# A written-out order of a sparse-attention and gMLP kernel replaced by another: order, engines, PSUM banks and transposes

## The chip, the cores and the metric

The kernel runs on one core of a Trainium2 chip. The metric is the device time of one execution in microseconds (us). Each engine (PE for matmuls, DVE, ACT, POOL for elementwise work, SP for starting transfers) takes its own queue of instructions strictly in order, and an instruction waits for those of other engines that it depends on. DMAs are started from queues as well: here from POOL's (loads that cast f32 to f16) and SP's (raw loads, transposing transfers inside SBUF, stores of the output).

## What is computed

Inputs are q, k, v of shape 4 x 8 x 768 x 64 (batch, head, position, width), and the weights of a gated MLP. The reference, cut to what matters:

```python
# attention; chunks of 32 keys, 24 chunks, the best 6 are kept for each query
k_min, k_max = np.min(k_chunks, axis=3), np.max(k_chunks, axis=3)
ub = np.sum(np.maximum(q[:, :, :, None, :] * k_min[:, :, None, :, :],
                       q[:, :, :, None, :] * k_max[:, :, None, :, :]), axis=-1)
ub = np.where(causal, ub, -1000000000.0)
top_chunks = np.argsort(ub, axis=-1)[..., -top_k:]
mask = sel & (pos[:, None] >= pos[None, :])
scores = np.where(mask, scale * np.matmul(q, k.transpose(0, 1, 3, 2)), -1000000000.0)
# softmax of scores, times v, heads put side by side: x of 4 x 768 x 512
h = np.maximum(x @ w_in, 0.0)                 # 512 -> 1024
u, v = h[..., :512], h[..., 512:]
v_n = (v - mu) / np.sqrt(var + 1e-06)
v_s = np.einsum('ts,bsd->btd', w_spatial, v_n) + b_spatial[None, :, None]
out = (u * v_s) @ w_out
```

## The kernel before

**Stages.** The 32 heads are taken as 16 pairs, 0 to 15; four pairs make a batch, two pairs share one "chunk" of loads (four heads of k and v, two loads of q). After every fourth pair the gMLP of that batch is mixed in with the attention of the next pairs. For a pair the stages are:

- `load_ops` (from L385): k, q and v are loaded by POOL's casting DMA (L414). For the first chunk each head of k and q can be loaded instead as raw f32 by SP (L419).
- `chunk_ops` (from L481): k of four heads is transposed to kT, on PE (L500, then a copy out of PSUM) or by one DMA transpose from SP (L488); raw f32 heads go through PE as f32 (L512). DVE takes the largest and smallest key of each chunk (L523, L526, L529).
- `put_ops` (L532): the chunk bounds are spread into km and the keys into kh, by copies on DVE (L249), POOL (L245) or ACT (L243).
- `prep_ops` (L549; `prep_first` for pair 0): q is transposed, on PE (L568) or by a DMA transpose from SP (L577). Two relu make rq, the positive and the negative part of q. If q went through PE, they read PSUM and run on DVE or ACT; if it went through the DMA they read SBUF, and run on DVE (L257, L259), POOL (L255) or ACT (L253). PE then multiplies rq by km: the upper bounds (L590, ten short matmuls). DVE finds the eight largest (L606) and writes a "not selected" mask beside q (L612). q and mask are transposed together to a, on PE (L626) or by DMA from SP (L617).
- `attend_ops` (L692): for each head and each of six strips, scores on PE (L711), exp on ACT (L722), then the causal triangle: added on PE as one more matmul (L714), or cut out afterwards on POOL (L733) or DVE (L731). PE multiplies by v (AV, L742), DVE normalises (L756), and x is transposed, on PE (L773) or by DMA (L766).
- `mlp_ops` (L778), once for each batch: the v half of the first layer (L790, 512 columns), relu, statistics (L796) and normalising (L814) of it, the u half (L832, 384 columns), the spatial product (L848, 384 columns), bias (L852), gates (L857, POOL or DVE), the last layer (L876, 512 columns), copies of it to `o` (ACT L243, DVE L247) and stores (L883). The very last tile of the output is made in two pieces of 256 columns.

**What sets the order.** Nothing is scheduled when the kernel is built. Every stage registers its operations by `s.op(...)`, with its engines to choose from, its PSUM bank if it takes one, and where there are two ways to do a thing, a "when" that belongs to one of them. The table PLAN (from L51) then says in which order they are issued. It is a string read three characters at a time:

```python
            hi, lo, how = (DIGITS.index(x) for x in plan[c:c + 3])
            o = self.ops[64 * hi + lo]
            if o.when is not None:
                assert self.mode.setdefault(o.when[0], o.when[1]) == o.when[1]
...
            if o.take is not None:
                o.take.tile = self.banks[how // 4 - 1]
            if len(o.alts) > 1:
                o.emit(list(o.alts)[how % 4])
```

Two characters name the operation, and the third gives the engine (remainder by 4) and one of eight PSUM banks. Listing one of two ways chooses it. The order of the table is the order on every engine's queue. The table was found by annealing on a planner's prices, which the code still carries beside each operation. The one for rq from SBUF, at L583, gives DVE 0.25, POOL 0.63 and ACT 0.62 us:

```python
                s.op([("DVE", 0.25, 0.37), ("POOL", 0.63, 0.7), ("ACT", 0.62, 0.76)], lambda e, m=m: relu(
                    e, rq[:, m, P:S].rearrange("p (t c) -> p t c", c=P), a[:, 1:NQT, 0, :], 1.0 - 2 * m), key + 0.2,
```

Of the kernel before, what the change touches and what calls it, by code (L numbers as in the profile page):

```python
# [37 lines left out]
def blocks(half):  # L38
# [10 lines left out]

DIGITS = "0123456789ABCDEFGHIJKLMNOPQRSTUVWXYZabcdefghijklmnopqrstuvwxyz+/"  # L50
PLAN = (  # L51
    "0000N10P10K10140I00D00t00S00H00O00o00V00800x00500B00v00600700U01880W10Z00900A00p00T00b00c10R1100"
    "0M00J10a14201200Q00d002C03G0E02dK0Y10z00C01901A00X01J11VO0F01B00w10L01C01KS1I11D01E004W1F02e02n4"
    "2h02j02+22i01hC2l01W11M01G11L04402z11Y01X01a04301f11H12k01g12o11j11Z01c08e01501b01N81i149G47K2r0"
    "1e01O02s02t01d11kO1P01Q01RW2u02m01l02w01m04A12v04811S13212y033S1n01o44J13001tC1y83513411qG4C01+0"
    "2x02/00k04B036K1p02KO4E08f01v04502TW4D02543701s02V04F02QS2S02F82H02CC3804G01/G3904PW5P04Q05WS2N8"
    "3113DK2M04R05Y04H03BO3C02108lG2P03E08jW2704M02E04I05X18k04L04S84T05T03I45S03NO3WC3K022K8g05O03Y0"
    "4K12403TS3V03FW3P05Z43oC3dK8m05U10j04N14U05a03rG3lS4V00G04X83q02JO5b02X0BB04O13H04ZC3n05R14Y03gW"
    "3Q85c05gS3f04a03i01x44jK3S02Y03uC8n02904bW3t08o03w05h04l08q00i0Fg05Q14m82A04o050G8p04zC5eS2Z00e0"
    "8r03MK3a03k84/04pO3b04d08s08u04eC3y05205V14r04g05EW8/G2B05G04sO3z05844u055C5A06IW5f0A9S6K08t03+0"  # L60
    "8+167O6903c0AA04i85r49008x0A508y08z140K5s0570910A204105BW4w00g06FO5D04x05x44y06H095G5y0960A810f0"
    "2bC6LK5jW5k0A10AB05+854O0h09705I08w1A6264SBI46N06CW5/05J08v16605mK9806E09AG9B15K0BJ0BC0AF85n09CO"
    "5uS6X42c09D06BWBGCAG0A715v09gO6P06Y09rGBH15MK5o05N16d46009s05pSA41BD0AH06Q0AI09h06109lC6R0BL09u8"
    "AJ06ZKA316e06208h09m06309v0FlWFm06bGFnO6a06c1BN09o49p09FC9G06f86TS9NW9O06U0ID0Fo0BK0BP09QG6VK6W1"
    "9T49R06iC9dS9e0BW17eWFq0BM076O6nK9WG9X07f09U0Fh0Ch16j06k07g06o0770Fi06g0BO0Ca07806sSFp06l0Fr06t0"
    "6u0BU06p0AqGBY8Ci4B2C7BW7C0B30Cj1ASOBa0AT07SSAnKAo0AXCBE0Ck0Cf0BR0Ce07T0BZ07U0Ar09Y06q07h8BQ0Ft0"
    "9I4BV0Cb0BeO9J06v07i0Fs07D06w0Bf0Cd1APK9w0AQ0CoS9i07VGFu0H806r07W0Cp06m0AY07X0H40714720Bg0730790"
    "6x0Bh07MW7bK7c07j0Cq0BX17N06y07E07407O09jC7A0AyGAz0Bi09x0Fv0AdOAe07Y4Fz0750Aa8Ab07Z07F0AgWAh07G0"
    "9K0Cg19LGCr0Fw06h06z06/06+09Z0BS17d0A/OB007PS7H0F+07007Q0G187a0G307R0Ai07I0AvWHBKAU0H70AVOAs0BT1"
    "Aw07L1Cc19a07J0Aj08747uS880G20HD09b07v0G7WHC1Ak07z8CAGAl07+07K1BoKCs0CB0Bp0BrO9y09z0Bs0G807/0890"  # L70
    "CDGBzCCRKH317w0G90Bt1COOFy0GA0Mi0F/1CE07pGB+07q0BwCB407r0CP0CS0IH0Bx0C/OFx08008HW7s00l0CLKGB08I0"
    "G01810D00CF1CM0C0CC10IE08J0At8CIOCJ0B50C3GC40DNKDO07x0HHC8K07t1B60DSSCT07kWDT0DYO9+0H61HI0DKGB70"
    "DVK7l07m0D48DZ082S8A0830DL0Db4CGOHJ0IN0HK0D50B9GH91HA1CU0IM0DW0DA87n0Dc0Dd1D7CDDKIF0840BA1HM4HN0"
    "CyWC50D80H51DB0BuGC60GSCCz0DE0GH8CV0DP08C47o08D0GtWIP0D10DQKCW0Mm0850Mk0HOOGT0GI0C70DF0De0Gu0C80"
    "HP0IO0GiCGj0GKSHR87y0GqGCX0Df0GYW8E0IQ0GL0GfOGnCDg00m08F0Fj0GZ0Gr0IR0IW0HfSGg0D2WIY1DG0DkKDH0HS0"
    "IT0IaGGo0Gk0DI0GP4GQ0IV1PF0Hg0Ic0DuOJk8Jd2Ib0Jm0HiWHj0Jc0DiCDj0IX1E84IZ1IU1HsGJl1GM0Ht0860DpSIS1"
    "Dv0Jg1IgCE90Ms0Ih0Ii0EjWI18Ek0Dw0Ij0Ik0Jh1GVGDl0Mj0EXOEY0EA0El0Dx0I20Gw4GW0HZWHa0Mu0Gx0Ga0Dm1Dq0"
    "Dr08PCMw08Q0PH0ER8JqGES0HcWH+KHx4GNSET0Hy0Gb0Hd08MCI48EZ18N0Ds0Jr0EgOMr0I50Dt0Js0Jt08B1Ju0Jj18O0"
    "Ji1Hk0Jf18L0Gl4HUWEh0HV0Ei0Je1EDGPJ0EB0EE0IqCEO8H/0Gy1Mt0Gc0Ir0EP0IG0ItWEQ0EF1Dn0J2OJ5KJ60Mv0J30"
    "Gz0I/GG+0M/1EUCMy0HW08G0E38Gd08R0J00Dy0Mx0Do0HpKG/0Hq0EaOJFSEG0IyGJG0E40Iz0Eb0I60N34JCKE51Ec0HXS"  # L80
    "JNGDz0D+0JO0EH0N40Hl0EV0N50EC0JK8Hm0JTOEW0JL08S4O50JU0D/0Hn0E10JD0N00Mz0JQG8T0N9CK9SJR0E60E70Hu0"
    "Hv8I70PG0N11EI0NA0E00K1OK208VKNB0Iu0EJ0OG0I80NC0JV08Y4JH0EdGEe0ND08W0EK0I90E21K6OKA0JIWK70Ef1EL0"
    "JW0EM0E/C8Z1EmKH00KF8ErGPP0Es0PR0PO0J70KaSKCOKG0En0M+1PQ0EN1J+8JX0F44JY0PW1KD0Eo0N21F50Kb0J/0Ep0"
    "F00KMOKdSPT0Ke0PS0KX8F10KN0O90F60KPWKQ0O62KY0Et0KH0K30K4SO818X0OB2IA0EwKEx0Ey0KUOEu0Iv0IwWNR8Eq0"
    "J80NJGKV0Ez0KR0F20FJK8a0J90Pf0JA0KI0OH2NpOJZ0OA2NS0F70NvCPY1Kf0FEWKJ0FF0PZ1KS8Kg0NK0OI1OJ4Qe0Nw0"
    "OC1Nq0NsG8U0KK0Kh0Ki0Kj0FK0FG0NaCOK0F30NXSFL0Nb0NMOOL0F98O71OM0PV1FA0NhCQj2FB0Ph28b4E+0Ev1Nt0NN0"
    "QmGNUOPa1FC0Pb1FM08c0FH0Qo0ON0Pg0Qh1NV0FO8PU2NkKQn1Nl0FP0Ny4FN1LlWKrONz0Qk1Lm0LTGPiKLU0Ln1LV1Km8"
    "Qi2Kn0Qf2Pj0Pk0Pl0Ko1Kp08d0FR4KwWOeGKs0Kt1Ml0NY0P0SQg1P10Of0FS1Kx0OkKL58L60Ni0OTSL70ObGLZOFUCNO0"
    "Oz4Kq0Ol0Oh8PX1Nc0Oc0La0OU0FV0LAKL80LB0N+0Ky1Ql1LQGNm1QsWKz0Oi0O+0Ku0P6SLFCFD0LG0Qt0Lb0LR0Kv0LW8"
    "LX0P70Ou4K+0K/0OrOLH0LC1FI0Qu0L90LD0L00Pm0Qv0Os0LE0OWSNPKOX0OY0Nd0LcCLd0LS1Q4OOv0Le0Q7WL10P3SQ14"  # L90
    "Ne0F80FW0Nf0LfGLg0FT0OZCQ50L20QVKQ80LiOLY1Qw0LI0LJ0Om0NnWN/0QM8P40P80Lj0Lk1QHSL41On0Oo0Op0FQ0QW0"
    "Q20Ow0FXKO00Ps4QN0PvOFd8Lh1QPCLK0L30QI0LL0Pt0QESPI0LM0O10QSGPw0Fe0LP0QT0LN0P+4P/0LO0FY1FaOLy8FZ0"
    "QF0QQ0Q90O20RBWOxGP90PA0Lz0L+0RW4LoSFb0PB0RHCR0KRC0Lp0ROOQX0RX0Px0R3GLq0R10M1WRR4Lr0RI0LtKLs0Lu0"
    "Lv0RS0RP0RECR40RfSRF0RZ4R50R8OQJ1MGGR90Ff0L/0M00Ra0Rc8QKCRd0Lw0RT0QY0RJ0PyKM20QZ0Qa0M30M40Rg0R6O"
    "QA0QB0MB4RK0RL0RU8Rh0QC0M50Ri0Rj0Rk0PC0SCCM6SLx0MH0MLWRoKRM0MM0MN0MO0MP1Ry8MC0M70Qb0MI0MJ0MD0ME0"
    "M80MWOMX1S7WRl0M90MQGSY4RtORu0MR0MY0Rp0Rv0Rq1MA0Rz0Rw0R+0R/0Rr0S00SD0Rx0Rs0SHSSI0SJ1SE0SF0SG0Fc0"
    "S10S20S30SZ0Sa0MS0S80MTGSSOS90SA0S50SB0MF0MK0MfKSK0SL0Sn8So0MU0MZCShSS41Mg0ST0Ma0Mc4MV0SM0SN0SbW"
    "Sc0S60SU0Mb0Mh0T3GSO0SP1SvKSR1SqCSi0Sw0SQ1S+OSr0Sx0Md0Sd1Sy0Sj0SVWSW0Ss0Se4TDST40T50S/0T00SX0St0"
    "Su1SkKTNWSl0T60T10T21TE0Sf0TF0Sp0Sz1TG0TO0T70TP0TSCTT0T88Sg0Sm0T90TH0TQ0TIGTJ0TK0TA0TVOMe0TU0TR1"
    "TYSTW0TL0TB0TZ0TX0Ta0TM0TC1ThWTbCTi0Tj0Tc0Td0Te4Tf0TkKTg0Tl0Tm0"  # L100
)


# [831 lines left out]
```

## Time and profile before

| | |
|---|---|
| runs of before | 194.24, 194.37, 194.5 us; median 194.37 |
| profiled execution, its own time | 194.3 us |
| its span (first to last instruction) | 192.6 us |
| matmuls, starts of two 128-column ones apart (median) | 56 ns |
| first score matmul (L711) starts | 15.68 us |
| last matmul ends; last store issued; landed | 188.98; 189.66; 191.55 us |
| stores of 256 KB, issue to landing | 2.2 us (median) |
| DMA transposes: a<-qs, xT<-x, kT<-kp | 12, 10, 3; 4.3, 2.6, 5.3 us to landing (median) |

How to read the profile: busy time is that of instructions on an engine, as a share of the span. The slices are 40 equal parts of the span, each digit the busy share in tenths; PEclk is the clock that PE was granted, in tenths of full speed. The chain of waits goes back from the last instruction to what released it, step by step. In groups, "out<-in" are the tiles' names, then shapes, how often, busy time and the mean of one in ns, and the idle time just before with what ended it. A timeline line has start, length, engine, line and operation; several instructions in a row are put together with their number.

### The profile page before, as it was taken

The page shows a single profiled execution, that of the slowest core. Times are in us where ns is not written, and L with a number is a line of the kernel's source. Part 1 is how long each engine was busy: PE and PEld are TensorE (multiplying, and loading weights), DVE is VectorE, ACT ScalarE, POOL GpSimd, SP SyncE. Part 2 cuts the span into 40 slices and gives each one's busy share as a digit, 9 for nine tenths or more (in the row PEclk, how much of TensorE's full clock was granted, in tenths as well). Part 3 has the DMA queues.
Part 4 walks back from the last instruction along what each step waited for, and adds up shares of the span by engine and source line. Part 5 has one row for each costly group of instructions (what it writes and reads, how often), then busy time and mean ns, then how long its engine had stood idle before and what let it go on. Part 6 is the DMA issues. An engine that isn't in the chain of part 4 may idle for free.

```text
span 192.6 us, 5740 instructions
## 1 busy us (share of the span) xinstructions
PE 183.5 (95%) x2132; PEld 130.4 (68%) x2132; DVE 157.3 (82%) x549; ACT 153.3 (80%) x326; POOL 129.1 (67%) x215
## 2 busy tenths in 40 slices
PE   7649999999999999999999999999999999999992
PEld 7548999997567677875667667655776775456541
DVE  5978999999699999899999988979987366674840
ACT  8998999999999899898889887849799810596052
POOL 7988899979967949999985478995173560500310
PEclk9975999999999999999999999999999999999999
DMA  8999999999996999999999968689359412423035
GB/s 126 136 153 158 166 148 162 188 175 162 156 127 133 156 197 158 127 150 141 180 213 172 162 188 137 177 85 120 116 134 147 129 38 46 167 99 119 0 122 205
DMA packets 111291, 27.33 MB, mean 142 GB/s; under 512 B 106144, under 2 KB 107680, under 8 KB 111264
## 3 DMA queue, kind: packets, MB, share of 16 engines
q0 software_dynamic: 73904, 11.90, 83.5%
q1 hardware_dynamic: 37360, 15.08, 34.1%
q8 instruction: 16, 0.26, 0.6%
q14 instruction: 11, 0.09, 0.1%
HBM read 24.77 MB, written 6.29 MB: 161 GB/s over the span
## 4 chain that ended last, share of the span: by engine, by line
PE 82%; DVE 8%; ACT 4%; POOL 2%; issue 2%; ACTq 0%; POOLq 0%; DVEq 0%
PE bank L711 18%; PE bank L848 16%; PE bank L876 10%; PE bank L790 10%; PE bank L742 10%; PE bank L832 8%; PE bank L590 2%; PE bank L626 2%; PE bank L568 2%; DVE st L796 2%; POOL kp L414 1%; PE bank L714 1%; ACT kh L243 1%; PE bank L773 1%; PE bank L500 1%
## 5 line engine op out<-in xcount | busy, mean ns | idle before, releaser
L722 ACT ACTIVATE e<-bank 128x512 f16<-128x512 f32 (+2 forms) x192 | 92.6, 558 | 11.2 <-PE bank L711 6.5
L711 PE MATMUL bank<-a,kh 128*128 128x128 f16 (+2 forms) x384 | 58.7, 263 | 0.2 <-DVE x L756 0.2
L711 PEld LDWEIGHTS <-kh 128*128 128x128 f16 x384 | 32.5, 99 | 11.9 <-issue 0.6
L857 POOL TENSOR_TENSOR shared<-tmp,uT 128x384 f16<-128x384 f32 x22 | 20.4, 935 | 28.6 <-DVE tmp L852 28.3
L848 PE MATMUL bank<-wsT,vn 128*128 128x384 f16 x192 | 39.2, 326 | 0.1
L245 POOL COPY kh<-kT 64x384 f16<-64x384 f16 x55 | 29.1, 530 | 7.5 <-PE bank L711 4.6
L733 POOL TENSOR_SCALAR_AFFINE_SELECT e<-e 128x384 f16<-128x384 f16 x44 | 23.3, 542 | 15.4 <-ACT e L722 14.0
L832 PE MATMUL bank<-xT,w_in 128*128 128x384 f16 x128 | 28.5, 326 | 0.1
L742 PE MATMUL bank<-vt,e 128*128 128x65 f16 x672 | 27.4, 193 | 0.0
L742 PEld LDWEIGHTS <-e 128*128 128x128 f16 x672 | 25.0, 97 | 2.3
L790 PE MATMUL bank<-w_in,xT 128*128 128x512 f16 x96 | 25.4, 379 | 0.0
L243 ACT COPY o<-bank 128x512 f32<-128x512 f32 x19 | 11.3, 594 | 17.5 <-PE bank L876 15.6
L876 PE MATMUL bank<-w_out,shared 128*128 128x512 f16 (+1 forms) x100 | 24.0, 371 | 0.1
L852 DVE TENSOR_TENSOR tmp<-bank,bias 128x384 f32<-128x384 f32 x32 | 17.1, 552 | 8.4 <-PE bank L848 6.3
L848 PEld LDWEIGHTS <-vn 128*128 128x128 f16 x192 | 17.1, 98 | 10.0 <-DVE vn L814 0.5
L756 DVE TENSOR_TENSOR x<-bank,rec 128x384 f16<-128x384 f32 x32 | 17.5, 551 | 0.5
L414 POOL DMA_DIRECT2D qs<-in_q_dram x17 | 17.2, 1009 | 0.1
L832 PEld LDWEIGHTS <-w_in 128*128 128x128 f16 x128 | 11.3, 97 | 7.8 <-issue 0.3
L796 DVE BATCH_NORM_STATS2 st<-vraw 128x6 f32<-128x512 f32 x24 | 16.0, 681 | 0.7 <-ACT vraw L253 0.6
L876 PEld LDWEIGHTS <-shared 128*128 128x128 f16 x100 | 9.4, 98 | 9.2 <-DVE shared L857 0.6
L606 DVE MAX8 m<-bank 128x8 f32<-128x8 f32 (+4 forms) x150 | 13.5, 164 | 0.1
L790 PEld LDWEIGHTS <-xT 128*128 128x128 f16 x96 | 8.7, 98 | 7.1
(99 smaller groups left out, 297.4 us busy)
## 6 DMA issues: line engine op xcount, KB each, us to landing
out_dram<-o SPq DMA_DIRECT2D x23, 256.0 KB, 2.2
vt<-in_v_dram POOLq DMA_DIRECT2D x8, 384.0 KB, 7.2
kp<-in_k_dram POOLq DMA_DIRECT2D x7, 384.0 KB, 7.1
qs<-in_q_dram POOLq DMA_DIRECT2D x14, 192.0 KB, 5.4
shared<-in_moe_w_spatial_dram POOLq DMA_DIRECT2D x3, 384.0 KB, 6.2
w_in<-in_moe_w_in_dram POOLq DMA_DIRECT2D x4, 256.0 KB, 6.4
w_out<-in_moe_w_out_dram POOLq DMA_DIRECT2D x2, 256.0 KB, 5.7
vraw<-in_k_dram SPq DMA_DIRECT2D x2, 192.0 KB, 2.7
```

Source lines behind the costliest of these rows:

```text
L245: nc.gpsimd.tensor_copy(o, f)
L414: s.op(("POOL", 0.62 + 0.19 * nh, 0), lambda: nc.gpsimd.dma_start(out=dst(name, h0, nh), in_=src(a, h0, nh)), key, w=w, load=PAIRB * nh / ...
L711: mm(bs.f32[:, col:col + n], lhsT=kh[:, hi, t * P:(t + 1) * P], rhs=a[:, f // P:(f + n) // P, hi, :], start=True, stop=not on)
L722: s.op(("ACT", *act_cost(n)), lambda g=g, n=n, bs=bs, e=e: nc.scalar.activation(out=e[:, BASES[g]:BASES[g] + n], in_=bs.f32[:, 0:n], func= ...
L733: nc.gpsimd.affine_select(out=o, in_=o, compare_op=Alu.is_ge, fill=0.0, base=0, channel_multiplier=-1, pattern=[[0, 3], [1, P]])
L742: mm(o[:, qi, :], lhsT=e[:, c:c + P], rhs=v_r[nv][:, 2 * hi + x, t, 0:D + 1], start=first and n == 0, stop=last and n == len(bl) - 1)
L790: mm(bk.f32, lhsT=x[:, ko, t * P:(t + 1) * P], rhs=w_in_sb[:, ko, DH:DFF], start=(ko == 0), stop=(ko == NDO - 1))
L796: s.op(("DVE", 0.60, 0.74), lambda vraw=vraw, st=st: nc.vector.bn_stats(st, vraw), kk, r=[("vr", nvr[t])], w=[("st", nst)])
L832: mm(bk.f32[:, 0:N], lhsT=w_in_sb[:, ko, db * P:(db + 1) * P], rhs=x[:, ko, c], start=(ko == 0), stop=(ko == NDO - 1))
L848: mm(bk.f32[:, 0:N], lhsT=vn[:, si, db * P:(db + 1) * P], rhs=wsT[:, si, c], start=(si == 0), stop=(si == NQT - 1))
L857: eng.tensor_tensor(gT[:, db, c], in0=tmp, in1=uT[:, db, c], op=Alu.mult)
L876: mm(bo.f32[:, 0:c1 - c0], lhsT=gT[:, db, t * P:(t + 1) * P], rhs=w_out_sb[:, db, c0:c1], start=(db == 0), stop=(db == KO - 1))
```

## The change

Only the string PLAN is replaced, from its first line to its last. No operation, shape, price or function changes; the table stays about as long. The first and last lines of the diff, which has 49 such lines on each side:

```diff
@@ -49,55 +49,55 @@
 PLAN = (
-    "0000N10P10K10140I00D00t00S00H00O00o00V00800x00500B00v00600700U01880W10Z00900A00p00T00b00c10R1100"
-    "0M00J10a14201200Q00d002C03G0E02dK0Y10z00C01901A00X01J11VO0F01B00w10L01C01KS1I11D01E004W1F02e02n4"
+    "0v00000H00N00o00I10140R00S00280V003C0800B00x00501100600C00t00K00M00W00700p04200D02dG0900Y10L00a1"
+    "0b00Z00Q00c01200T00d10P00z00U10O143018K0w22pO0J11911J11VS2e00A02h02j02l02i01KW0E00F00442q11h82k0"
...
```

What the two tables come to, counted on each engine:

| operation | before | after |
|---|---|---|
| K transposes on PE (L500); f32 ones (L512) | 54; 6 | 39; 9 |
| K chunks by DMA (L488) | 3 | 4 |
| q transposes on PE (L568); pairs by DMA (L577) | 78; 2 | 60; 5 |
| a transposes on PE (L626); pairs by DMA (L617) | 60; 10 | 48; 11 |
| triangles on PE (L714); POOL (L733); DVE (L731) | 42; 44; 6 | 54; 37; 9 |
| rq from SBUF on POOL (L255) | 1 | 6 |
| rq from PSUM on DVE by L259 | 13 | 7 |
| gates on POOL; on DVE (L857) | 22; 10 | 20; 12 |
| copies of o on ACT (L243); on DVE (L247) | 19; 4 | 14; 9 |
| uT relu on ACT; on DVE | 23; 9 | 19; 13 |
| raw k loads from SP in the front (L419) | 2 | 3 |

The order of nearly all operations is new as well, and so are the banks. At the start, SP loads q2, k0, k3, k2 in place of k2, k0, q2; the mask rows of L371 (ACT) are made by L373 (DVE); the 54 matmuls on a zero tile that begin PE's queue (L343) are grouped differently. At the end, the last piece issued is a tile of 512 columns that DVE copies, in place of a piece of 256 columns that ACT copies.

## The prediction

> **What bounds the kernel now.** I read the page's share of busy time and its slices first, then the chain of waits, then the costliest groups by form, then single tiles. Page, busy time, slices and chain of before:
>
> ```profile
> PE 183.5 (95%) x2132; PEld 130.4 (68%) x2132; DVE 157.3 (82%) x549; ACT 153.3 (80%) x326; POOL 129.1 (67%) x215
> ...
> PE   7649999999999999999999999999999999999992
> ...
> POOL 7988899979967949999985478995173560500310
> PEclk9975999999999999999999999999999999999999
> ...
> PE 82%; DVE 8%; ACT 4%; POOL 2%; issue 2%; ACTq 0%; POOLq 0%; DVEq 0%
> ```
>
> PE is full from the fourth slice to the last but one: between 20 and 186 us PE is busy 165.6 of 166.0 us in the table of stretches. Outside lie a front of about 15.7 us (first score matmul L711 at 15.68) and a tail (last matmul ends at 188.98, last store lands at 191.55). So the time is front + PE's own work + PE's stalls + tail. For the work I use the distance between starts of two matmuls of a kind, read in the trace (median ns): 56 for 128 columns, 109 for 256, 162 for 384, 216 for 512, 29 for an AV step, 25 for an upper-bound step L590. Times all matmuls this gives 179.2 us; from 20 to 189 us PE loses only 2.7 us over it, nowhere more than 0.33 us at once. So a saved PE instruction in the body is worth its distance, and a stall of PE is worth its length, if nothing later swallows it.
>
> **The change, part by part.** Only PLAN is new: every matmul, copy and load is of the same shape. The two programs' orders, engine by engine, give the differences.
>
> *PE work.* Twelve K transposes (L500, one chunk), 18 q transposes (L568, pairs to DMA L577: 2 to 5) and 12 of the selected q (L626, one pair to DMA L617: 10 to 11) leave PE: 42 x 0.056 = 2.35 us. Twelve triangle matmuls L714 come (seven POOL triangles L733 less; DVE's L731 rise 6 to 9): 12 x 0.056 = 0.67. Net **-1.68 us**. The three L500 that become three L512 in the front are in the front's term.
>
> *POOL's rq.* A pair whose q goes through the DMA transpose gets its two relu (rq) as SBUF to SBUF work, on DVE, POOL or ACT. Before has one on POOL; after has six: pair 12 two, 13 two, 14 one, 15 one. The groups by form of before:
>
> ```profile
> L255 POOL TENSOR_SCALAR rq<-a 128x640 f16<-128x640 f16 x1 | 2.3, 2349 | 0.0
> ...
> L257 DVE TENSOR_SCALAR rq<-a 128x640 f16<-128x640 f16 x1 | 0.5, 473 | 0.0
> ```
>
> The planner's price at L583 for POOL is 0.63 us, DVE 0.25, ACT 0.62. The row says 2.35: the plan was annealed as though POOL had 1.72 us more at each of the six. I price POOL's queue by rows (kh copy 0.50, km 0.20, triangle 0.54, gate 0.92, q load 1.04, rq 2.35). In the 50 us of PE work from 50 to 100 (PE's distances added up; clock time is this plus 8 to 9), POOL's load goes from 38.2 to 51.8 us: it is over full there. I lay POOL's queue end to end from 86.75, where it is behind two gates that DVE's L852 has just released. It runs gate, km, gate, kh, triangle, kh, km, gate, rq 2.35, triangle, q load 1.04, rq 2.35, km twice. The second rq of pair 12 ends at about 98.0 on PE's axis, and PE's L590 of pair 12 stands at 96.9: **1.1 us** of stall. Then q load, three triangles, km, rq, kh, rq: the last rq of pair 13 ends at about 105.9 against L590 at 104.2, so 1.7 us late from the same origin; 1.1 of it has been paid, so 0.6 is new. Stalls on one queue don't add: the total is the largest lateness, **1.7 us**. For pairs 14 (116.6) and 15 (120.8) POOL is about on time. Behind the late L590 on PE stand scores of the pair before and spatial matmuls that need nothing of it; PE takes its queue in order, so they wait too. The same laying for before's only POOL rq is my check:
>
> ```profile
> 116.92 2.35 POOL L255 TENSOR_SCALAR rq<-a 128x640 f16<-128x640 f16 x1
> 119.11 0.51 PEld L590 LDWEIGHTS <-rq 128*128 128x128 f16 x10
> 119.14 0.58 PE L590 MATMUL bank<-km,rq 128*128 128x48 f16 x10
> ```
>
> (Timeline: start, length, engine.) It put the end of that rq 0.10 us ahead of L590; in the trace it ends at 119.27 with L590 at 119.14, a loss of 0.157 us. So the laying errs a little on the early side: POOL was 0.05 to 1.1 us later than laid. Bounds of this term: 0 (POOL has worked ahead of its place by 1.7 us when it comes to pair 12, or its earlier entries wait less) to 3.0 us (late by 1.1 more, and a later tile inherits some).
>
> A rule speaks against this term. The Trainium skill's "GPSIMD Engine Reference", section 4.1, holds one-input elementwise work on GpSimd to be roughly line rate; with its 1.03 cycles an element (section 3.1) at 1.2 GHz, 640 elements would be an estimated 0.55 us. By that price the term would be nothing and the sum some 193.5 us. The row of this case, 2.35 us, decides.
>
> *Front.* First loads on SP go from k2, k0, q2 to q2, k0, k3, k2; POOL's small loads from five to four. Up to the second select of pair 0 (L674), row prices give ACT 12.65 instead of 15.09 us of work, but DVE 10.79 instead of 9.93 (it takes the mask rows L373 and a cast). The chain of before runs through ACT there:
>
> ```profile
> 11.19 0.51 ACT kh L243
> 11.69 0.38 ACT kT L243
> 12.07 1.19 ACT rq L253 x2
> 13.54 0.42 PE bank L656 x10
> ```
>
> ACT's relief would pay, but it is followed by DVE, which has four K chunks' reductions (two L523 of 0.25, two L526 of 0.20, two L529 of 0.24 each) ahead of the first L656. Ends: +0.86 (all DVE's addition shows) and -0.9 (POOL's last q load goes one issue earlier, 0.85 to 1.04 us by its row, and all else follows). The walk entry by entry gives a first score at 16.4 instead of 15.7, less 0.4 because L590 of pair 1 now stands ahead of it: I take **+0.3**. The slow clock (slices 3 and 4, 11.65 to 18.48 us) I expect unchanged.
>
> *Tail.* Timeline of before:
>
> ```profile
> 189.11 0.38 ACT L243 COPY vraw<-bank 128x256 f32<-128x256 f32 x1
> 189.66 0.38 SPq L883 DMA_DIRECT2D out_dram<-vraw  x1
> ```
>
> The last piece is a half-width one, copied by ACT in 0.38 and landed in 1.9 us. After has a full-width piece last, copied by DVE (row 128x512 o<-bank: 0.685 us) and stored in 2.0 to 2.2 us: +0.31 and +0.1 to +0.3. PE's wait for the last gate (0.24 at 185.7) is some 0.13 longer by the same laying. Total 0.4 to 0.7, **+0.5**; nothing covers it, as no work is left.
>
> *DMA transposes.* One more kT, three more q, one more a through SP. Rows of before for issue to landing: a<-qs 3.2 to 6.3 us, kT 3.3 to 5.7, xT 2.6. From issue to first use, on PE's axis, pair 11's q has 5.1 us, 12's 5.5, 13's 3.6, 14's and 15's 2.3 and 2.9, pair 14's a 5.3, 15's 6.0. For 13 to 15 the first user is POOL's rq, which by the laying comes 2 to 3 us after its place, so these landings (4.3 to 5.4 by the two L577 of before) are hidden under the same lateness and not paid twice. Ends: 0, and 1.0 (a landing of 6.3 against the 5.3 of pair 14's a). I take **0**, since from 100 to 150 us, where it stands, the DMA share is 0.97 against 1.51 in the 50 us before. The Trainium skill ("Trainium Kernel Development and Optimization", Key Constraints) says that all queues' DMAs interleave on the same 16 engines; the 3.2 against 6.3 us for one kind fits that, and with such a long landing at pair 14 the sum would be 196.2.
>
> *Other moves.* DVE's copies of o (4 to 9), uT (9 to 13) and gates (10 to 12) against fewer rq (13 to 7) and vn leave DVE and ACT near 80%, with ends of their entries no later against PE than before's by the same laying (up to 1 us in both): 0, ends -0.3 to +0.5. POOL in pairs 1 and 2 is laid up to 2.7 us late for a kh tile where before has under 1: POOL's queue is behind weight and v loads. I take nothing for it because the front's term already carries the start, and keep +0.7 as its end.
>
> **Sum**, on the profiled execution (194.3 us, span 192.6, so 1.7 around the span): -1.68 + 1.7 + 0.3 + 0.5 = +0.82, that is 195.1; the median of the runs shown is 194.37, and from there **195.2 us**.
>
> **Rivals.**
>
> *A, POOL keeps up.* The six rq hide behind an earlier POOL, as the plan wants; PE's saving shows. For it: POOL is 67% busy over the span, and between 105 and 112 us it idles 3.36 us at once. Against it: 51.8 us of work in 50 by rows, and two rq back to back ahead of one L590. -1.68 + 0.3 + 0.5 = -0.9: 193.5 us; with the front's gain instead of its loss 192.7 (-0.5 there). It decides if POOL comes to the first rq of pair 12 more than 1.7 us ahead of its laid place (PE axis 91.4, about 100 us on the clock).
>
> *B, POOL's lateness spreads.* Slower by more: the lateness before pair 12 is 1.1 us over the laying, as before's worst entries were; kh copies and triangles queued behind the four rq hold up the scores and AV of pairs 11 to 13, and the early POOL end (+0.7) is paid too. +0.82 + 1.1 + 0.7 = 197.0 us. It decides from the point where POOL comes to the first rq of pair 12 later than 1 us after its laid place.
>
> *C, nothing to be seen.* The new lengths buy nothing: half the POOL term hides (0.85), and what PE saves goes back into front and tail: -1.68 + 0.85 + 0.8 = 0.0, 194.4 us.
>
> **Chances.** Forecast (194.8 to 196.2) 0.41; B 0.15; C 0.17; A 0.27. Within 0.2% means 193.98 to 194.76 us, about what a measurement of this kernel can tell from no change: faster 0.27, same 0.17, slower 0.56. The range must take in most of A and B: 192.9 to 197.1. The slower cases alone give 194.8 to 197.1.
>
> **What would show it.** PE's busy time falls by about 1.7 us; six L255 on POOL of about 2.35 us, most of them between 96 and 130 us; L590 of pairs 12 and 13 (between 104 and 115 us) with idle time of PE ahead of it, released by POOL rq; first L711 near 16.0; last store landing about 2.6 us after PE's last matmul plus copy. The forecast is wrong if L255 is well under 2 us when it has neighbours, if POOL reaches pair 12's first rq ahead of its laid place, or if the front moves by more than 0.9 us either way.

## The result, and the profile after

| | before | after |
|---|---|---|
| median (runs) | 194.31 us (4: 193.9 to 194.5) | 205.38 us (4: 204.53 to 207.46) |
| profiled execution, span | 194.3, 192.6 us | 205.33, 203.6 us |
| ratio, 95% interval | | 1.0589 [1.0508, 1.0669] |

Every ratio here leaves out runs more than 1.5% above the fastest of the same kernel, so it need not be the quotient of the medians beside it, and where one run is left none is given.

The change made the kernel 11.1 us slower. The forecast had the sign, but the time lies 8.3 us above the range's upper end. PE has less to do and still ends 11 us later, so I first look for where it idles. The page of after (busy time, slices of 5.09 us, shares of the chain):

```profile
PE 184.4 (91%) x2102; PEld 128.7 (63%) x2102; DVE 163.8 (80%) x560; ACT 147.1 (72%) x309; POOL 136.2 (67%) x212
...
PE   7779999986999997698996897889999999999992
...
POOL 7999998978849798937899989789512206100230
PEclk9979999999999999969999999999999999999999
DMA  7999999999999999999999998973953051025045
...
PE 46%; DMA 18%; POOL 15%; DVE 11%; issue 5%; ACT 4%; POOLq 0%; DVEq 0%
```

PE, full from the fourth slice on before, has holes from the ninth to the 27th slice (41 to 137 us) and is full again only after them. In the chain PE falls from 82% to 46%, and DMA, which had no share large enough to be listed, has 18%. POOL rises from 2% to 15%. The row that the prediction passed over is that of the DMA engines. In the page of before it reads:

```profile
DMA  8999999999996999999999968689359412423035
```

Even before the change the 16 DMA engines are 90% busy or more in nearly every slice up to 110 us. After it the stretch reaches to 122 us without a break. The longest waits of PE in after (engine, line, releaser: us in total, times, longest; those of L500 are in the front, before 20 us), and four of them in the timeline (start, length; the bracket holds the idle time ahead and who ended it):

```profile
PE bank L711 <- DMA a<-qs: 3.2, 2, 2.0
PE bank L711 <- issue: 2.2, 1, 2.2
PE bank L568 <- DMA qs<-in_q_dram: 2.0, 1, 2.0
PE bank L500 <- DMA kp<-in_k_dram: 1.5, 2, 1.3
PE bank L590 <- POOL rq L255: 1.5, 1, 1.5
```

```profile
51.19 0.49 PE L568 MATMUL bank<-identity,qs 128*128 128x128 f16 x6 [1.97 <-DMA qs<-in_q_dram]
...
86.18 0.60 PE L711 MATMUL bank<-a,kh 128*128 128x256 f16 x5 [2.02 <-DMA a<-qs]
...
112.50 0.38 PE L711 MATMUL bank<-a,kh 128*128 128x384 f16 x2 [2.16 <-issue]
...
123.65 0.40 PE L590 MATMUL bank<-km,rq 128*128 128x48 f16 x9 [1.50 <-POOL rq L255]
```

The first is a plain q load and the second the DMA transpose of a selected q. For the third the profile names no releaser, but a transpose a<-qs issued at 102.33 us landed at 112.42, just ahead of it. Only the fourth is the wait that the forecast was built on. The chain of waits (start, length, what) shows how long those transfers were under way:

```profile
37.60 1.03 POOL qs L414
38.63 12.42 DMA qs<-in_q_dram
...
71.31 8.35 DMA a<-qs
...
84.71 9.72 DMA kT<-kp
...
112.09 5.78 DMA a<-qs
118.05 2.56 POOL rq L255
...
121.25 2.35 POOL rq L255
```

A q load of 192 KB that took 4.1 to 6.9 us to land before takes 12.4 us here; the two transposes a<-qs on the chain take 8.4 and 5.8 us and kT<-kp 9.7. It is so with most kinds of transfer (the stores stay at 2.2 us), as the lists of DMA issues show (KB each, median us from issue to landing), first before's, then after's:

```profile
vt<-in_v_dram POOLq DMA_DIRECT2D x8, 384.0 KB, 7.2
kp<-in_k_dram POOLq DMA_DIRECT2D x7, 384.0 KB, 7.1
qs<-in_q_dram POOLq DMA_DIRECT2D x14, 192.0 KB, 5.4
...
kT<-kp SPq DMA_TRANSPOSE x3, 5.3
```

```profile
vt<-in_v_dram POOLq DMA_DIRECT2D x8, 384.0 KB, 10.0
kp<-in_k_dram POOLq DMA_DIRECT2D x7, 384.0 KB, 8.9
qs<-in_q_dram POOLq DMA_DIRECT2D x14, 192.0 KB, 7.9
...
kT<-kp SPq DMA_TRANSPOSE x4, 9.1
```

**Where the 11.0 us of span lie.** Matmuls by kind times the distance of their starts give PE's work; the rest of PE's time is waits and slow clock.

| | forecast | measured |
|---|---|---|
| PE's work, 179.2 to 177.6 us | -1.68 | -1.57 |
| PE's loss up to 20 us, 5.8 to 4.1 | +0.3 | -1.7 |
| PE's loss from 20 us on, 2.7 to about 16.4 | +1.7 | +13.7 |
| last matmul to end of span, 3.61 to 3.94 | +0.5 | +0.3 |

The rows add up to +10.7; 0.3 us of the 11.0 I can't place. Of the 16.4 us, 11.4 are nine idle times of 0.55 to 2.16 us between 45 and 136 us, 1.7 a window of half clock, and the rest is idle time in pieces under 0.3 us. Transfers ended five of the nine, 8.0 us together: a w_in load (0.66), the q load (1.97) and three a<-qs (1.19, 2.02, 2.16). The POOL gap at 122 us is 1.5, and DVE ended the other three (1.9 together).

### The profile page after: what moved, and what is told of

Read it like the earlier page. It is cut to its first block, busy times and chain, and to the rows that moved or that the text cites. A ratio compares the mean times of both kernels' runs of the same rounds, so it can differ in the third digit from the quotient of the medians.

```text
span 203.6 us, 5686 instructions
## 1 busy us (share of the span) xinstructions
PE 184.4 (91%) x2102; PEld 128.7 (63%) x2102; DVE 163.8 (80%) x560; ACT 147.1 (72%) x309; POOL 136.2 (67%) x212
## 4 chain that ended last, share of the span: by engine, by line
PE 46%; DMA 18%; POOL 15%; DVE 11%; issue 5%; ACT 4%; POOLq 0%; DVEq 0%
PE bank L848 11%; PE bank L832 8%; PE bank L711 8%; PE bank L876 7%; DMA a<-qs 7%; DMA qs<-in_q_dram 6%; PE bank L790 6%; POOL kh L245 5%; DMA kT<-kp 5%; PE bank L742 4%; POOL rq L255 2%; POOL qs L414 2%; POOL km L245 2%; ACT rq L253 2%; DVE st L796 1%
## 5 line engine op out<-in xcount | busy, mean ns | idle before, releaser
L711 PE MATMUL bank<-a,kh 128*128 128x128 f16 (+2 forms) x384 | 58.6, 261 | 6.6 <-DMA a<-qs 3.2
L711 PEld LDWEIGHTS <-kh 128*128 128x128 f16 x384 | 32.3, 98 | 20.3 <-issue 4.7
L848 PE MATMUL bank<-wsT,vn 128*128 128x384 f16 x192 | 38.4, 326 | 0.0
L857 POOL TENSOR_TENSOR shared<-tmp,uT 128x384 f16<-128x384 f32 x20 | 18.0, 911 | 28.0 <-DVE tmp L852 26.7
L245 POOL COPY kh<-kT 64x384 f16<-64x384 f16 x53 | 27.8, 525 | 7.3 <-PE bank L711 4.8
L733 POOL TENSOR_SCALAR_AFFINE_SELECT e<-e 128x384 f16<-128x384 f16 x37 | 21.1, 583 | 15.4 <-ACT e L722 14.3
L832 PE MATMUL bank<-xT,w_in 128*128 128x384 f16 x128 | 27.9, 326 | 0.0
L790 PE MATMUL bank<-w_in,xT 128*128 128x512 f16 x96 | 26.1, 383 | 1.3 <-DVE qs L612 0.7
L742 PE MATMUL bank<-vt,e 128*128 128x65 f16 x672 | 26.7, 193 | 0.1
L876 PE MATMUL bank<-w_out,shared 128*128 128x512 f16 (+1 forms) x100 | 24.9, 380 | 0.1
L253 ACT ACTIVATE vraw<-bank 128x512 f32<-128x512 f32 x16 | 9.6, 600 | 12.7 <-PE bank L790 12.5
L414 POOL DMA_DIRECT2D qs<-in_q_dram x17 | 17.2, 1019 | 0.0
L832 PEld LDWEIGHTS <-w_in 128*128 128x128 f16 x128 | 11.4, 98 | 6.9
L255 POOL TENSOR_SCALAR rq<-a 128x640 f16<-128x640 f16 x6 | 14.4, 2403 | 1.5 <-DMA a<-qs 1.4
L245 POOL COPY km<-kmm 64x24 f16<-64x24 f16 x47 | 10.7, 230 | 5.7 <-issue 3.4
```

Source lines behind the costliest of these rows:

```text
L245: nc.gpsimd.tensor_copy(o, f)
L255: nc.gpsimd.tensor_scalar(o, in0=f, scalar1=sign, scalar2=0.0, op0=Alu.mult, op1=Alu.max)
L414: s.op(("POOL", 0.62 + 0.19 * nh, 0), lambda: nc.gpsimd.dma_start(out=dst(name, h0, nh), in_=src(a, h0, nh)), key, w=w, load=PAIRB * nh / ...
L711: mm(bs.f32[:, col:col + n], lhsT=kh[:, hi, t * P:(t + 1) * P], rhs=a[:, f // P:(f + n) // P, hi, :], start=True, stop=not on)
L733: nc.gpsimd.affine_select(out=o, in_=o, compare_op=Alu.is_ge, fill=0.0, base=0, channel_multiplier=-1, pattern=[[0, 3], [1, P]])
L742: mm(o[:, qi, :], lhsT=e[:, c:c + P], rhs=v_r[nv][:, 2 * hi + x, t, 0:D + 1], start=first and n == 0, stop=last and n == len(bl) - 1)
```

## The experiments

The letters in the expectations stand for these theories. **P**: POOL's six rq alone. **V**: the five v loads to which after gives 6 to 28 us more lead, alone. **T**: the transfer time of the five added DMA transposes, alone. **TL**: transposes and changed loads together. **D**: the DMA engines are what bounds this stretch, so that work added to them, or less lead for a load, is paid. **O**, **L** and **K** are told where they come. "Lead" is PE's work between the place where a transfer is issued and its first use. The edits are to entries of PLAN, given as operations unless the entry itself is short; medians, and ratios to before's runs of the same call (its medians 193.9 to 194.6) with 95% intervals.

### Undoing parts in after

`a_rq_dve`: the six rq go back to DVE, by the last digit of their entries.

```diff
-N71 N81 OH1 OI1 Pg1 Qq1
+N70 N80 OH0 OI0 Pg0 Qq0
```

> After's table with the six rq of pairs 12 to 15 on DVE in place of POOL, nothing else moved. Theory T (the 16 DMA engines are full until about 110 us, and five more transposes through them push every landing back): POOL's rq is no cause, 203.5 to 205.5 us. Rival P (POOL's six rq of 2.4 us hold up the upper bounds, as forecast): 196 to 199 us. Rival V (v loads issued up to 20 to 30 us earlier stand ahead of urgent transfers): as T, 203.5 to 205.5.

Measured 204.31 us, but its four runs spread from 199.19 to 207.16, so no interval is given and the gain is unclear; the fastest run comes to the edge of P's range. Its profiled run was the slowest. In that profile POOL's rq is gone from the waits, and PE waits 7.0 us in six places for a<-qs, where after has 3.2 in two. P as the whole cause doesn't fit after's own waits, of which only 1.5 us are POOL's; that the wait moved to the transfers is read from this one profile.

`a_5_on_pe`: K chunk 3, a of pair 9 and q of pairs 11, 12 and 15 are transposed on PE as in before.

```diff
-L488 kT of chunk 3; L617 a of pair 9; L577 q of pairs 11, 12, 15
+L500 x12; L626 x12; L568 x18; their copies
```

> After's table with the five transposes that it newly gave to the DMA (K chunk 3, selected q of pair 9, q of pairs 11, 12 and 15) back on PE, and their copies and relu on DVE and ACT; loads stay where they are. 1.8 MB less goes through the DMA. T: about 1.5 MB of it stands in the full stretch, at some 150 KB/us 9 us, less 1.8 us of PE work: 196 to 199 us. P: three of the six POOL rq are gone, 200 to 202. V: 204 to 207, PE's added work shows and the v loads still stand in front.

Measured 212.11, ratio 1.0924 [1.0867, 1.0981]: some 7 us slower than after, not faster. Besides 42 x 0.056 = 2.35 us of PE work, it brought new waits at the transposes that I put in (L500 0.75 and 0.36, L568 0.66 and 0.50 us), and it has gaps of 2.0 to 2.5 us at L711, L832 and L590. As a repair it failed; it also can't clear the transposes, since the order around them was made for having them on the DMA.

`a_v_late`: v loads of chunks 3 to 7 get before's leads.

```diff
-ldv3..7 leads 29.9 24.3 29.5 36.1 13.8 us
+ldv3..7 leads 21.1 10.6 10.5 7.9 7.9 us
```

> After's table with the five later v loads (chunks 3 to 7) moved back, to the same lead over their first use as in before (21, 11, 10, 8 and 8 us of PE work instead of 30, 24, 30, 36 and 14). The five transposes stay on the DMA. V: 196 to 199 us. T: the same bytes must go through before the matmuls of pair 13, less what now moves behind 110 us (768 KB at 150 KB/us, 5 us at most), 200 to 205. P: no change, 205.

Measured 207.24, 1.0672 [1.0633, 1.0712]. V alone falls: with these loads later it is no faster than after, and the chain still has the DMA at 21%.

`a_both`: both of the last two edits.

> Both edits: five transposes back on PE and the five v loads late. T and V both expect 194.5 to 197 us, T with most of it from the transposes, V with most of it from the loads (to be read beside the two kernels with one edit). P: 200 to 202.

Measured 214.33, 1.1022 [1.0966, 1.1077], far from the 194.5 to 197 that T and V both expected.

`a_leads`: k and q loads of after get before's leads (chunk 5's k 10.1 to 23.3, a q of chunk 5 4.3 to 12.8, of chunk 7 11.1 to 25.2 and so on), and v loads before's later ones.

> After's table with the loads of k, q and v moved to before's lead over their first use, counted in PE work: eleven k and q loads earlier by 1 to 14 us (q of chunks 5, 6 and 7 from 4 to 11 us of lead back to 12 to 25), five v loads later. The five new DMA transposes stay. Theory L (after gives its loads a lead shorter than the 8 to 12 us in which they land on a full DMA, so PE waits for data): 196 to 200 us. Theory T (the bytes of the added transposes are what costs): 203 to 206 us. Both know that putting the transposes back on PE alone did not help (212 us).

Measured 210.24, 1.0801 [1.0729, 1.0874]. It is above both expectations. Its first scores came 1.6 us later, and a q load landed so late that L568 waited 4.1 us at 53 us. `a_leads_pe` has the five transposes on PE as well:

> After's table with both edits: the five transposes back on PE, and the k, q and v loads at before's leads. Neither alone helped (212 and 210 us). Theory TL (two halves of one fault: more DMA work due by a given point of PE's queue, 132 instead of 117 us of it by PE work 130, and loads with too little lead): 195 to 199 us. If something else in after's order costs (front, PE order, engines of DVE and ACT): 203 us or more.

Measured 212.30, 1.0915 [1.0869, 1.0962]. TL, as far as after could show it by undoing, isn't borne out. `a_k3_pe` puts only K chunk 3 back on PE:

> After's table with K chunk 3 alone back on PE, 384 KB less on the DMA from 32 us on. TL: the DMA is relieved by 2.4 us early, the short leads stay: 203 to 206 us. Theory K (a DMA transpose beside the big weight loads is what stops the DMA, as for 15 us in the four-transposes kernel): 197 to 201 us.

Measured 209.17, 1.0758 [1.0706, 1.0810], with the same two new waits at L500; neither TL nor K has it. Undoing parts in an order that was annealed as a whole thus costs new waits each time, and such runs tell little. So the same parts were put into before, whose PE from 20 us on never waits more than 0.33 us at once.

### Parts of the change, one at a time in before

`b_leads_qk`: eleven k and q loads of chunks 3 to 7 get after's leads; nothing else moves.

```diff
-ldk4 14.3; ldk5 23.3; ldk6 11.5; ldq5 12.8; ldq6 11.7, 20.8; ldq7 11.5, 25.2; ... us ahead
+ldk4  9.7; ldk5  9.9; ldk6  9.3; ldq5  4.0; ldq6  4.2,  7.3; ldq7  8.8, 10.6; ... us ahead
```

> Before's table with the k and q loads alone at after's shorter leads; v loads stay where they are. L: 199 to 205 us, and nearly the same as with the v loads moved too if the short leads are the cause; 194 to 197 if the early v loads ahead of them are what makes them late. T: 194 to 196.5.

Measured 198.23 (196.64 to 200.0), 1.0133 [1.0098, 1.0168]: +2.6 us by the ratio, which is in the range set down for "the early v loads are what makes them late" and not in L's. The profile has PE gaps of 0.75 us at L711 (65.4 us) and 1.70 at L568 (101.8 us); a q load landed 5.7 us after its issue, with 4.2 us of work ahead of it.

`b_leads`: v loads of chunks 3 to 7 moved ahead to after's leads as well.

> The mirror image: before's table with the k, q and v loads of chunks 3 to 7 moved to after's leads (eleven of k and q later, five of v earlier), nothing else touched; no transpose is moved. L: 200 to 206 us. T: 194 to 196.5, since no byte is added.

Measured 206.30, 1.062 [1.0585, 1.0655]: +12.0 us, with no added DMA work, no added transpose and POOL's rq as before. On the chain stand a<-qs at 8.0 and 11.8 us, xT<-x at 8.4 and a q load at 6.5, and PE's four waits over 0.5 us (0.79, 2.19, 2.08 and 2.47) each end within 0.15 us after one of these landings. Two windows of half clock, 3.41 us each, come on top. My reading is that early v loads and late q and k loads crowd into the same stretch, and what is needed first lands last.

`b_k3_dma`: one K chunk more (chunk 3) by the DMA transpose.

```diff
-BGC BH1 BI4 BJ0
+BF0
```

> Before's table with K chunk 3 alone on the DMA, beside the w_in loads. K: 202 to 206 us, with the 9 us gap of PE at L464 seen with four transposes. TL: bytes alone, 194 to 197 us.

Measured 206.11, 1.0529 [1.0445, 1.0613], +10.3 us for one transpose of 384 KB. The chain, then the table of stretches from 33 to 53 us (busy time of PE, PEld, DVE, ACT, POOL, granted clock, DMA share, GB/s), of before and of this kernel:

```profile
32.36 20.24 DMA kT<-kp
```

```profile
33.00:53.00 20.00, 20.00 (x305) 16.30 (x303) 17.30 (x60) 19.27 (x40) 18.09 (x33) 1.00 1.87 171
```

```profile
33.00:53.00 20.00, 11.60 (x208) 10.31 (x206) 8.40 (x39) 10.52 (x22) 10.56 (x21) 0.79 1.53 110
```

The transpose starts beside the loads of w_in and takes 20.24 us to land; the median of w_in's landings goes from 6.4 to 17.6 us. The engines move 110 instead of 171 GB/s in these 20 us, at a share of 1.53 against 1.87. A standing PE asks for less, but that isn't all of it: from 37 to 42 us, while PE was still full, they moved 108 against before's 200 (before's line first):

```profile
37.00:42.00 5.00, 5.00 (x110) 4.77 (x107) 4.79 (x25) 4.85 (x11) 3.77 (x8) 1.00 1.27 200
```

```profile
37.00:42.00 5.00, 4.98 (x100) 4.34 (x97) 4.26 (x20) 4.63 (x10) 4.42 (x8) 1.00 1.41 108
```

PE then idles 4.2 us at L500 and 4.2 at L711, and its clock is at half from 44.7 for 13.65 us. By the ratio this is in K's range (202 to 206), and far above what TL expected of the bytes alone.

`b_3_on_dma`: a of pair 9 and q of pairs 12 and 15 by the DMA.

```diff
-L626 x12 for pair 9; L568 x12 for pairs 12, 15
+L617 for pair 9; L577 for pairs 12, 15
```

> Before's table with the selected q of pair 9 and q of pairs 12 and 15 on the DMA, without K chunk 3: 1.1 MB more, 6.7 us of DMA work, where before has 15 to 20 us of room by PE work 110. TL: 196 to 201 us. K: 193.5 to 196, no big load runs beside them.

Measured 201.84, 1.036 [1.0315, 1.0406], +7.0 us, just above TL's range and well above K's. Chain and waits:

```profile
75.64 6.42 DMA a<-qs
...
101.26 8.00 DMA a<-qs
```

```profile
PE bank L590 <- DVE rq L257: 5.2, 1, 5.2
...
PE bank L711 <- DMA a<-qs: 1.7, 1, 1.7
```

Pair 12's q was issued 3.8 us before PE came to its L590 (at 105.0 us) and landed in 8.0 us; rq waits for it, L590 for rq, and PE stands 5.2 us, after which the clock is at half for 6.83 us. The first releaser by name is DVE; the chain shows that DVE itself waited for the transfer. Pair 15's transpose, at 124 us where the DMA has room, caused no gap.

`b_4_on_dma`: these three and K chunk 3.

> Before's table with four of the five transposes put on the DMA (K chunk 3, selected q of pair 9, q of pairs 12 and 15; pair 11's is left, as its tile comes free only 2 us ahead of its use), their relu on DVE. 1.5 MB more through the DMA, 1.3 us less PE work, loads as in before. T: 199 to 203 us. L: 193.5 to 197, a wait of 1 to 2 us at the most where a lead is 4.6 to 5.4 us.

Measured 212.07, 1.0824 [1.0773, 1.0875], +16 us, about the two parts together (10.3 + 7.0) and above every expectation; kT<-kp takes 21.1 us to land and PE stands 8.9 us at 42 us.

### Less for the DMA to do, with after's order untouched

`a_tiny5` cuts the five added transposes to one block of 128 columns each; the rest of kT and a keeps old data, so the output isn't the reference's:

```diff
-                out=kT.rearrange("p h (t c) -> p (h t) c", c=P), in_=...), key,
+                out=kT.rearrange("p h (t c) -> p (h t) c", c=P)[:, 0:1 if n == 3 else 12], in_=...), key,
...
+            nb = 1 if i in (11, 12, 15) else 2 * NQT - 1
...
+            out=a.rearrange("p t h c -> p (t h) c")[:, 0:1 if i == 9 else 12], in_=...
```

> After's table, untouched; the five transposes newly given to the DMA move one block of 128 columns instead of 11 or 12, so the rest of their target keeps old data and the output is not the reference's. 1.7 MB, some 10 us of DMA work less, no instruction moved. Theory D (the DMA engines have more work due than they can do): 196 to 200 us. Theory O (the order of after itself is too tight, whatever is moved): 203 to 206.

Measured 204.50 (201.3 to 208.7), 1.0436 [1.0347, 1.0524]. T alone falls: with nearly all of their bytes gone, the median is 0.9 us lower; by the ratios the difference is 3 us with overlapping intervals. Either way it is short of the gain that D expected (196 to 200).

`a_tiny_v` loads one tile of six of v, chunks 3 to 7, and leaves out the other five:

```diff
+            if a is v and n >= 3:
+                return a[b, h + h0:h + h0 + nh, 0:P].rearrange("h p d -> p h d")
```

> After's table, untouched; the v loads of chunks 3 to 7 bring one of six tiles (64 KB of 384), so that most of v is old data. 1.6 MB, some 10 us of DMA work less. D: 196 to 200 us, as for the transposes, since it is the sum that counts. O: 203 to 206. If only transposes beside loads are what is slow: 202 to 205.

Measured 202.78 (199.3 to 205.8; no interval given). `a_tiny_both` has both cuts:

> After's table with both sets of transfers shrunk (five transposes and five v loads), 20 us of DMA work less. D: 193 to 196 us: PE's smaller work less POOL's rq. O: 201 or more.

Measured 202.18, 1.0407 [1.033, 1.0484]. Some 20 us of the DMA engines' work (an estimate from packet rates in the trace: five transposes at 2.2 us each, and 1.6 MB of loads less at about 154 KB a us) brought 3.2 us. By what was set down this is O's case (201 or more: the order is too tight, whatever is moved) and not D's (193 to 196): the amount of DMA work isn't the whole of the bound. What is left still waits for transfers, now in a bunch between 52 and 76 us, and for POOL. `a_tiny_both_rq` moves the six rq to DVE as well:

> As before this one, with the six rq of POOL on DVE. With the DMA out of the way this shows what POOL's rq cost by themselves. Forecast's term: 1.7 us less than with them on POOL. If POOL has room: within 0.4 us of it.

Measured 197.61, 1.0181 [1.0113, 1.0249]: 4.6 us less than `a_tiny_both` by the medians, 4.4 by the ratios. With the transfers relieved, the same edit that did nothing clear in `a_rq_dve` pays. The two waits covered each other. The chain of this kernel still holds two transfers one behind the other:

```profile
51.25 1.37 POOL vt L418
52.62 12.29 DMA kp<-in_k_dram
64.96 11.81 DMA kT<-kp
```

The k load that the transpose needs is issued behind a v load and lands in 12.3 us, and its transpose needs 11.8 more. (The added lines shift the numbers: L418 is L414 of after.) So the amount of work (D) is a part of it, and the order in which the transfers stand counts at least as much (O).

### POOL's rq alone, and a transpose where there is room

`b_rq_pool`: before's four rq of pairs 13 and 14, on ACT, POOL, DVE and ACT, all on POOL.

```diff
-OH2 OI1 Pg0 Ph2
+OH1 OI1 Pg1 Ph1
```

> Before's table with the four rq of pairs 13 and 14 all on POOL (two were on ACT, one on DVE, one on POOL), 7 us of POOL work more between 115 and 130 us, where POOL is 85 to 95% busy in before; DMA untouched. If each POOL rq costs what after shows (4.6 us for six): 195.5 to 197 us. If only a POOL queue that comes late anyway makes them costly: 194 to 195.

Measured 199.52 (199.41 to 199.77), 1.0276 [1.0253, 1.0299]: +5.4 us for three more rq on POOL, more than either expectation had, at a place where the DMA has room (a share of 0.72 to 1.06 from 115 to 135 us in before). The timeline:

```profile
118.98 2.33 POOL L255 TENSOR_SCALAR rq<-a 128x640 f16<-128x640 f16 x1
...
124.66 2.35 POOL L255 TENSOR_SCALAR rq<-a 128x640 f16<-128x640 f16 x1
...
126.97 0.91 POOL L857 TENSOR_TENSOR shared<-tmp,uT 128x384 f16<-128x384 f32 x1
...
128.97 2.57 POOL L255 TENSOR_SCALAR rq<-a 128x640 f16<-128x640 f16 x1
```

```profile
121.37 0.40 PE L590 MATMUL bank<-km,rq 128*128 128x48 f16 x9 [2.03 <-POOL rq L255]
...
127.94 0.60 PE L876 MATMUL bank<-w_out,shared 128*128 128x512 f16 x2 [1.44 <-POOL shared L857]
...
131.59 0.42 PE L590 MATMUL bank<-km,rq 128*128 128x48 f16 x10 [1.37 <-POOL rq L255]
```

Two gaps are L590 waiting for its rq; the middle one is a gate of POOL (L857) that stood in POOL's queue behind an rq. They add up to 4.84 us: lateness is caught up between them and paid anew.

`b_q15_dma`: only pair 15's q by the DMA, its rq on DVE.

```diff
-QmG Qo0 QnK
+Qp0 Qr0 Qq0
```

> Before's table with the q transpose of pair 15 alone on the DMA, issued 6 us of PE work ahead of its use, at about 130 us, where the DMA is no longer full; its two rq on DVE. PE saves six transposes, 0.34 us. If DMA work is free there: 193.4 to 193.9 us. If a transpose costs time anywhere: 195 or more.

Measured 193.64 (12 runs, 193.4 to 194.21) beside 194.04 for before (17 runs), 0.9976 [0.9962, 0.9990]. It is the one version that beats both kernels, by 0.4 to 0.5 us. PE loses six transposes (6 x 0.056 = 0.34 us by its rows) and has no gap; the transpose is issued at 124.40 us, 6 us ahead of its use, where the table of before has a DMA share of 0.84 (125 to 130 us) against 1.47 to 1.81 from 20 to 100 us. The same DMA transpose that cost 5 us of stall at 101 us for pair 12 is a gain here.

## Why the prediction was right or wrong

**PE's work: right.** -1.57 us against -1.68.

**Front and tail: right within their ends, small.** The first score starts at 15.46 (forecast about 16.0, before 15.68). The larger part of the front's -1.7 is that the half clock lasted 3.41 instead of 6.83 us; `b_leads_qk`, whose front is before's, shows 3.41 as well, so this varies between runs and isn't the change's. The last copy takes 0.69 us on DVE as the row said, and the tail grew by 0.3 instead of 0.5.

**POOL's rq: right mechanism, too small.** All six take 2334 to 2547 ns (forecast 2.35 us), and L590 waits for them. The group of after, where the time just ahead is POOL's own wait:

```profile
L255 POOL TENSOR_SCALAR rq<-a 128x640 f16<-128x640 f16 x6 | 14.4, 2403 | 1.5 <-DMA a<-qs 1.4
```

In after only 1.5 us of PE idling is POOL's directly. That this is close to the 1.7 forecast is luck: it stands ahead of pair 13 alone, with nothing at pair 12, where 1.1 was forecast; POOL's rq were themselves late for their transposes (the 1.4 above), and PE was late too. With the transfers relieved the term is 4.4 to 4.6 us (`a_tiny_both_rq` against `a_tiny_both`), and three of them cost 5.4 in before. The failing part of the working is "stalls on one queue don't add: the total is the largest lateness". In `b_rq_pool` they add (2.03 + 1.44 + 1.37), since POOL catches up between them while PE's next need has its own due time.

**The step that failed: "DMA transposes ... I take 0", with ends 0 and 1.0, and loads not priced at all.** The working compared leads of after with landings read in before (3.2 to 6.3 us), as if a landing belonged to the transfer. It belongs to the load on the engines. The DMA row of before, at 9 until 110 us, said that they had little to spare there, and I read the share only from 100 to 150 us, "where it stands". Of the five added transposes one stands there: after issues K chunk 3 at 31.9 us, a of pair 9 at 75.5, q of pairs 11 and 12 at 90.1 and 98.4, and only q of pair 15, at 134.0, behind 100 us. K chunk 3 and a of pair 9 weren't among the leads that I compared; a of pair 9 took 10.5 us to land, and the wait of 2.02 us above is for it. The table of stretches from 50 to 125 us (DMA share last but one), before and after:

```profile
50.00:75.00 25.00, 24.81 (x290) 17.20 (x289) 23.16 (x95) 22.95 (x52) 19.00 (x40) 1.00 1.56 163
75.00:100.00 25.00, 24.84 (x315) 17.69 (x314) 23.50 (x75) 22.42 (x47) 22.96 (x35) 1.00 1.47 152
100.00:125.00 25.00, 25.00 (x299) 17.44 (x298) 23.06 (x76) 20.81 (x48) 18.27 (x31) 1.00 1.10 167
```

```profile
50.00:75.00 25.00, 23.81 (x303) 17.68 (x304) 21.59 (x89) 22.37 (x49) 19.69 (x34) 1.00 2.02 174
75.00:100.00 25.00, 20.96 (x224) 13.47 (x222) 18.98 (x57) 17.05 (x38) 18.43 (x29) 0.93 1.89 149
100.00:125.00 25.00, 21.35 (x251) 14.28 (x249) 19.43 (x72) 18.69 (x42) 23.33 (x27) 1.00 1.61 177
```

The share adds up the times of all packets, so it goes over 1 where several are under way on an engine at once. It rises by 0.4 to 0.5 everywhere, while the GB/s stay within 11 of before's: more is under way on the engines, and hardly more is moved. Over the first 100 us the two kernels move 157 and 159 GB/s, so nearly the same; but counted from the two tables, some 2 MB more is due in after for the first 100 us of PE's work (an estimate from the sizes in the DMA lists). Of the order's moved loads the prediction said nothing beyond POOL's issue time, though the new PLAN shows them: a q load of chunk 5 with 4.3 us of lead instead of 12.8, of chunk 6 with 4.2 instead of 11.7, behind v loads issued up to 28 us earlier. The rule quoted from the Trainium skill, that all queues' DMAs share the same 16 engines ("Trainium Kernel Development and Optimization", Key Constraints), was the right one and was weighed against one landing only; the runs bear it out (one transpose from SP, and POOL's w_in loads land in 17.6 instead of 6.4 us).

**Rivals.** A (POOL keeps up) and C fell. B had the direction, POOL's lateness spreading, but not the larger cause and 8 us too little. No rival had the transfers as the bound; the range could not reach what none of its cases held.

**What is settled and what isn't.** Shown, each alone in before: leads of k and q loads +2.6; with the v loads +12.0; one K transpose beside w_in's loads +10.3; three q and a transposes +7.0; three rq on POOL +5.4. So moves and transposes of this kind, each by itself, cost as much as the whole change or a good part of it. Shown in after: less DMA work and rq on DVE together take 205.4 to 197.6. Not settled is how the 11 us divide: the parts overlap, after issues its K transpose 3.4 us ahead of three loads of w_in, not behind one as `b_k3_dma` does, and it lands in 8.4 us there; and each undoing in after brought waits of its own. That a shorter order of transfers would remove the last 3.7 us of `a_tiny_both_rq` is argued from its chain and wasn't run.

## What to carry to other kernels

Read the DMA row before any lead is judged: where it stands at 9, a landing time from the old trace is a property of the old load, and every added transfer, and every load moved ahead or back, can cost PE a wait as long as its lead is short. Price a moved load by its lead against the longest landing of its kind in a full stretch, and give a case of the range to that bound. When undoing a part of an annealed order brings its own waits, add the part to the old order instead; and take two waits that cover each other apart together (rq back alone: unclear; with the DMA relieved: 4.6 us).

## What the runs showed of the hardware

- A DMA transpose and casting loads can slow each other down by much. In `b_k3_dma` the transpose was issued 1.3 us behind the first of four w_in loads and took 20.2 us to land (21.1 in `b_4_on_dma`), where the three of before take 3.2 to 5.7; from 37 to 42 us 108 GB/s were moved against 200. In after, with three of these loads issued 3.4 to 5.1 us behind it, it took 8.4. Why is open.
- PE can fall back to half clock after short idle times in mid-kernel. In after, gaps of 1.19 and 2.02 us at 78 and 84 us are followed by this (stretch, busy times, clock):

```profile
87.60:91.00 3.40, 3.40 (x13) 1.50 (x11) 1.73 (x4) 2.33 (x6) 0.89 (x3) 0.50 1.63 206
```

  Not every such gap does it: after's own 2.16 us at 110 us and the three of 1.37 to 2.03 in `b_rq_pool` are followed by none, and what decides is open. The windows are 3.41, 6.83 or 13.65 us long, so a wait can be paid about one and a half times (in `b_3_on_dma` 5.2 us and then up to half of 6.83). The Trainium skill ("TensorE: Matmul & The Clock Gate", HAM oscillation) warns of idle gaps above some 3.4 us; here a window came with no gap over 2.02 us ahead of it.
- Kernels that wait for transfers vary by 0.6 to 4% between runs (`b_leads` 205.3 to 206.6, after 204.5 to 207.5, `a_rq_dve` 199.2 to 207.2), before by 0.5% (193.8 to 194.8 in 17 runs).
- DMA engines whose row stands at 9 moved 149 to 177 GB/s over 25 us and more in before and after, in packets nearly all under 512 bytes (106,144 of 111,291 in before). The Trainium skill's "DMA: Bandwidth & Descriptors" (Bandwidth, Measured) has 341 GB/s for a 1 MB load; by that figure, as an estimate, the stretch would have half its room left. The rows decide.
